# Sketch attention and causal experts on one core: TensorE's order written out, normalisation moved to the values, two sketch matmuls made one

## The chip, the cores and the metric

The kernel runs on one core of a Trainium2 chip. The metric is the device time of one execution in microseconds (us), the median of several runs. TensorE does matrix products and transposes, VectorE (DVE) and ScalarE (ACT) do reductions, exponentials and the copies out of PSUM, GpSimd (POOL) does small elementwise work in SBUF, and DMAs are issued by SyncE's queue and ScalarE's.

## The reference

There are four batches of 1088 tokens. A first part makes x from sketches of q and k, a second part runs four causal attention experts on x and mixes two of them for each token:

```python
phi(x) = outer(S1 x, S2 x)                 # 8 x 8 = 64 features, per head (4 heads of 32)
kv, z  = phi(k).T @ v, sum(phi(k))
x      = (phi(q) @ kv) / (phi(q) @ z + 1e-6)          # heads side by side: 128 wide
logits = x @ w_gate;  w = softmax over the two largest
for e in range(4):
    q, k, v = x @ wq[e], x @ wk[e], x @ wv[e]         # 64 wide
    a  = softmax(causal(q k.T / 8))                   # a / (a.sum() + 1e-9)
    out += gate weight of e * (a @ v @ wo[e])
```

S1 and S2 are float64 in the inputs. The kernel splits each into a nearest float32 (hi) and the rest (lo).

## The kernel before

All matrix products are float32. The program shows each such product as two MATMUL instructions, a transpose as one.

**First part of a batch** (`sketch_attention`, lines 216 to 268). k and q are brought to [128 = 4 heads x 32, tokens] by VectorE. `features` makes, for each of 9 chunks of 128 tokens, two accumulating products with the hi and the lo sketch (L200, 64 columns each), copies one half out of PSUM (L204) and lets VectorE multiply the halves (L209). `kv` is a sum over the chunks with two heads in one product (L236). Then follow, in three groups of three chunks, transposes of phi(q) (L246), their copy to SBUF, the numerators and denominators (L252), the division (L257 to L259) and transposes to xT (L264).

**Projections** (`project`, lines 271 to 315). Four products of 1088 columns for q and k of the experts (L277, L279), nine for v and the logits (L288), and the gate's weights on VectorE.

**Experts** (`experts`, lines 417 to 441). The 1088 queries are nine tiles: eight of 128 and a last one of 64. The steps run over groups of tiles (0 to 3, 4 to 7, 8), pairs of experts g and tiles i. `weights` (L321) makes the scores of two experts e (L336; each uses 64 of the array's rows), adds the causal mask by a product (L339), takes the row maximum (L345), scales it (L348), the exponential with its sum (L351), and multiplies the weights by gate over sum (L358 to L360). `turn_weights` (L372) transposes them in chunks of four, each chunk into one PSUM bank and out again by `evacuate` (lines L67 on VectorE, every third, and L69 on ScalarE). `values` (L385) multiplies them with v for up to 512 queries, the two experts at different columns of the array, and `output` (L396) applies wo.

**Order.** The loop at the end (lines 443 to 459) emits `weights` of a step, `turn_weights` of the step before, and one piece of the next batch's first part and projections. The framework's scheduler then orders each engine's instructions itself, TensorE's too. Of the eight PSUM banks, scores have two tiles of two banks, `tp` two banks and `o` two.

Of the kernel before, what the change touches and what calls it, by code (L numbers as in the profile page):

```python
# [9 lines left out]
F32 = mybir.dt.float32  # L10
# [8 lines left out]
def kernel(  # L19
# [37 lines left out]
    ps_o = ctx.enter_context(tc.tile_pool(name="ps_o", bufs=2, space=bass.MemoryType.PSUM))  # L57

    def const(name, shape, dt=F32):
        return cp.tile(shape, dt, name=name, tag=name)  # L60

# [9 lines left out]
    # ---- buffers of the first part: a batch's loads follow the reads of the one before it  # L71
# [8 lines left out]
    glog = const("glog", [128, NJ, E])  # L80
# [14 lines left out]
    # ---- the sketches: rows (S1, S2) at each head's partitions  # L95
# [8 lines left out]
    else:  # L104
# [9 lines left out]
        # The words of a float64, as a sum of two float32: the nearest one, and the rest. Both come  # L114
        # from its leading 24 bits, which are a float32, and its last 29.
# [38 lines left out]
    SK = []  # L154
    for n, s_sb in enumerate(sketches):
        ST = const(f"ST{n}", [128, 32])
        SK.append(const(f"SK{n}", [128, 2, H, R]))
        nc.vector.transpose(ST, s_sb)
        nc.vector.memset(SK[n], 0.0)
        for h in range(H):  # L160
            rows = slice(32 * h, 32 * h + 32)
            nc.vector.tensor_copy(SK[n][rows, :, h, :], ST[rows, 0 : 2 * R].rearrange("d (x r) -> d x r", x=2))  # L162
    NS = len(sketches)

# [5 lines left out]
    nc.gpsimd.memset(glog, 0.0)  # L170

    # ---- constants and weights of the second part
# [8 lines left out]
    for e in range(1, E):  # L181
        nc.gpsimd.memset(lower[:, e, 0:e], 1.0)

# [10 lines left out]
    # ---- first part of a batch, in pieces: x of its tokens, transposed  # L194
    def features(b, nm, xT_):
        """The products of two sketches, tokens on partitions; tokens that pad give zeros."""
        ab = ps_sc.tile([128, 1024], F32, tag="sc", name=f"{nm}ab{b}")
        for j in range(NJ):
            for s in range(NS):
                nc.tensor.matmul(ab[:, 64 * j : 64 * j + 64], xT_[:, 128 * j : 128 * j + 128],  # L200
                                 SK[s].rearrange("p x h r -> p (x h r)"), start=(s == 0), stop=(s == NS - 1))
        ab = ab[:, 0 : 64 * NJ].rearrange("p (j x m) -> p j x m", x=2, m=H * R)
        fa = p2.tile([128, NJ, H * R], F32, tag="fa", name=f"{nm}a{b}")
        nc.scalar.copy(fa, ab[:, :, 0])  # L204
        fp = p2.tile([128, NJ, H, R * R], F32, tag="fp", name=f"{nm}p{b}")
        fa4 = fa.rearrange("p j (h r) -> p j h r", r=R)
        fb4 = ab[:, :, 1].rearrange("p j (h r) -> p j h r", r=R)
        for h in range(H):
            nc.vector.tensor_tensor(  # L209
                out=fp[:, :, h].rearrange("p j (x y) -> p j x y", y=R),  # L210
                in0=fb4[:, :, h, None, :].to_broadcast([128, NJ, R, R]),
                in1=fa4[:, :, h, :, None].to_broadcast([128, NJ, R, R]),
                op=ALU.mult)
        return fp

    def sketch_attention(b, xT):
        n = NJ - 1
        nc.gpsimd.tensor_copy(vp[:, 0:n, :, 0:D].rearrange("p j h d -> p h j d"), vin)
        nc.gpsimd.tensor_copy(vp[0:64, n, :, 0:D], vtl)
        # Chunk j of k is the tokens that v has at vp[:, j]: c = j, n + j, 2 * n + j and 3 * n + j.  # L220
        nc.vector.transpose(kT[:, 0 : 128 * n].rearrange("p (j g t) -> p j g t", j=n, g=4),
                            kin[:, 0 : 128 * n].rearrange("p (g j d) -> p j g d", g=4, j=n))
        nc.vector.transpose(kT[:, 128 * n : S], kin[:, 128 * n : S])
        nc.vector.transpose(qT[:, 0:S], qin)
        if b + 1 < B:
            load(b + 1)
        kp = features(b, "k", kT)
        yield
        qp = features(b, "q", qT)
        yield  # L230

        kv = ps_o.tile([128, 512], F32, tag="o", name=f"kv{b}")
        kv = kv[:, 0 : 4 * (D + 1)].rearrange("p (m h d) -> p m h d", m=2, h=2)
        for m in range(2):
            for j in range(NJ):
                nc.tensor.matmul(kv[:, m], kp[:, j, 2 * m : 2 * m + 2, :].rearrange("p h f -> p (h f)"),  # L236
                                 vp[:, j, 2 * m : 2 * m + 2, :], start=(j == 0), stop=(j == NJ - 1))
        for h in range(2):
            nc.scalar.copy(kvz[64 * h : 64 * h + 64, :, h, :], kv[64 * h : 64 * h + 64, :, h, :])
        yield  # L240

        for g in range(NJ // 3):
            tq = ps_sc.tile([128, 1024], F32, tag="sc", name=f"tq{b}_{g}")
            for y in range(6):
                x, m = divmod(y, 2)
                nc.tensor.transpose(tq[:, 128 * y : 128 * y + 128],  # L246
                                    qp[:, 3 * g + x, 2 * m : 2 * m + 2, :].rearrange("p h f -> p (h f)"), ident)
            qpT = p2.tile([128, 6, 128], F32, tag="qpT", name=f"qpT{b}_{g}")
            evacuate(qpT.rearrange("p y s -> p (y s)"), tq[:, 0:768])
            num = ps_o.tile([128, 512], F32, tag="o", name=f"num{b}_{g}")  # L250
            for y in range(6):
                nc.tensor.matmul(num[:, 66 * y : 66 * y + 66], qpT[:, y], kvz[:, y % 2].rearrange("p h d -> p (h d)"),  # L252
                                 start=True, stop=True)
            nu = num[:, 0 : 12 * (D + 1)].rearrange("p (m d) -> p m d", d=D + 1)
            den = p2.tile([128, 12], F32, tag="den", name=f"den{b}_{g}")
            xs = p2.tile([128, 3, 128], F32, tag="xs", name=f"xs{b}_{g}")
# [5 lines left out]
            tx = ps_tp.tile([128, 512], F32, tag="tp", name=f"tx{b}_{g}")  # L262
            for x in range(3):
                nc.tensor.transpose(tx[:, 128 * x : 128 * x + 128], xs[:, x], ident)  # L264
# [3 lines left out]
            yield  # L268

    # ---- projections and gate of a batch, in pieces  # L270
    def project(b, xT, qk, vt, gw):
        tail = ps_o.tile([128, 512], F32, tag="o", name=f"qkt{b}")
        for a in range(2 * NG):
            w = wqk[:, a // NG, 2 * (a % NG) : 2 * (a % NG) + 2, :].rearrange("p e d -> p (e d)")
            t = ps_sc.tile([128, 1024], F32, tag="sc", name=f"qk{b}_{a}")
            for c in range(2):
                nc.tensor.matmul(t[:, 512 * c : 512 * c + 512], w, xT[:, 512 * c : 512 * c + 512],  # L277
                                 start=True, stop=True)
# [211 lines left out]
```

## Time and profile before

| | |
|---|---|
| median of three runs | 732.28 us (727.87 to 733.38) |
| span of the profiled execution | 731.8 us |
| TensorE busy | 632.2 us, 3012 matmul instructions |
| TensorE weight loads busy | 396.9 us |
| VectorE busy | 373.3 us |
| ScalarE busy | 231.1 us |
| GpSimd busy | 7.2 us |
| mean granted TensorE clock | 0.80 |

The span is from the first to the last instruction of one execution. The page gives no other time for that execution, and the span is within 0.1% of the median of the runs, so a sum made against the span can be read as one against the median. Busy times are unions over an engine; matmuls overlap one another in the array, so a busy TensorE isn't one at its peak. The granted clock is a share of 2.4 GHz and takes two levels, 0.5 (1.2 GHz) and 1.0.

### The profile page before, as it was taken

Reading aid. Unit: us, or ns where it says so; the run is one execution under the profiler, and the core shown is the slowest. Engines: PE = TensorE matmul, PEld = TensorE weight load, DVE = VectorE, ACT = ScalarE, POOL = GpSimd, SP = SyncE. Lnnn points to the kernel's source line nnn. Section 1 sums busy time; section 2 is a strip of 40 time slices with the busy share of each in tenths; the row PEclk is TensorE's granted clock in tenths of the full one; section 3 lists DMA queues with packets and bytes.
Section 4 is the critical chain, followed back from the end, with each engine's and each line's share of the span. In section 5 each row is a group of like instructions: output and inputs, shape, how many; then the busy total and the mean of one; then the engine's idle time right before and its main releaser. Section 6 shows DMA issues by size and latency. Waiting matters only on the chain.

```text
span 731.8 us, 8068 instructions
## 1 busy us (share of the span) xinstructions
PE 632.2 (86%) x3012; PEld 396.9 (54%) x3012; DVE 373.3 (51%) x1107; ACT 231.1 (32%) x555; POOL 7.2 (1%) x26
## 2 busy tenths in 40 slices
PE   3988999999878999898879899999888887888696
PEld 2965866554435885554434687554443553544345
DVE  4425454566563235658672334546755345574622
ACT  0022123343342113434341412344433333343413
POOL 1000000000000000000000000000000000000000
PEclk9989557999688555999987655999967867898885
DMA  7110110000000000000000000000000000000000
GB/s 211 57 36 1 46 47 1 0 15 0 1 0 15 3 1 0 1 14 1 1 0 1 16 1 1 1 3 12 1 1 0 15 3 0 16 0 1 0 11 6
DMA packets 11318, 9.97 MB, mean 14 GB/s; under 512 B 3600, under 2 KB 10256, under 8 KB 11280
## 3 DMA queue, kind: packets, MB, share of 16 engines
q1 hardware_dynamic: 9152, 8.92, 4.1%
q10 hardware_dynamic: 2128, 0.54, 0.4%
q8 instruction: 24, 0.39, 0.2%
q14 instruction: 14, 0.11, 0.1%
HBM read 7.23 MB, written 2.23 MB: 13 GB/s over the span
## 4 chain that ended last, share of the span: by engine, by line
PE 77%; DVE 11%; ACT 8%; issue 2%; DMA 1%; SPq 0%; ACTq 0%; DVEq 0%
PE sc L336 22%; PE av L385 14%; PE tp L372 12%; DVE mx L345 5%; ACT a L351 4%; PE qk L277 4%; PE qab L200 4%; PE kv L236 4%; PE kab L200 4%; ACT aT L69 3%; PE po L396 3%; PE num L252 3%; PE sc L339 2%; PE vg L288 2%; PE tq L246 2%
## 5 line engine op out<-in xcount | busy, mean ns | idle before, releaser
L336 PE MATMUL sc<-qkT 64*128 64x512 f32 (+3 forms) x448 | 195.1, 643 | 44.5 <-ACT a L351 44.2
L345 DVE TENSOR_REDUCE mx<-sc 128x1 f32<-128x128 f32 (+8 forms) x144 | 112.4, 804 | 141.8 <-PE sc L339 104.8
L372 PE MATMUL tp<-ident,a 128*128 128x128 f32 (+1 forms) x720 | 134.1, 326 | 25.9 <-ACT aT L69 17.0
L69 ACT COPY aT<-tp 128x256 f32<-128x256 f32 (+4 forms) x159 | 70.1, 449 | 205.9 <-PE tp L372 204.0
L351 ACT ACTIVATE a<-sc,mx 128x128 f32<-128x128 f32 (+8 forms) x144 | 112.0, 782 | 73.0 <-DVE mx L348 52.6
L372 PEld LDWEIGHTS tp<-ident,a 128*128 128x128 f32 (+1 forms) x720 | 95.7, 175 | 66.9 <-ACT aT L69 30.6
L336 PEld LDWEIGHTS sc<-qkT 64*128 64x128 f32 (+1 forms) x448 | 71.5, 212 | 101.8 <-ACT a L351 61.1
L385 PE MATMUL av<-aT,vt 128*64 128x64 f32 (+5 forms) x672 | 108.3, 443 | 1.5 <-DVE mx L348 1.5
L360 DVE TENSOR_SCALAR a<-a,z,gw 128x128 f32<-128x128 f32 (+8 forms) x144 | 86.8, 604 | 3.6
L385 PEld LDWEIGHTS av<-aT,vt 128*64 128x64 f32 (+1 forms) x672 | 54.1, 179 | 50.3 <-issue 37.3
L67 DVE COPY aT<-tp 128x512 f32<-128x512 f32 (+4 forms) x81 | 41.4, 511 | 38.1 <-PE tp L372 36.5
L200 PE MATMUL kab<-SK,kT 128*128 128x64 f32 x144 | 28.9, 389 | 16.6 <-DVE SK L162 12.6
L339 PEld LDWEIGHTS <-identb 128*128 128x128 bf16 (+1 forms) x144 | 11.0, 101 | 50.4 <-issue 47.9
L200 PEld LDWEIGHTS kab<-SK,kT 128*128 128x128 f32 x144 | 28.0, 300 | 17.5 <-DVE SK L162 12.8
L277 PE MATMUL qk<-xT,wqk 128*128 128x512 f32 x64 | 33.0, 638 | 0.9 <-issue 0.9
L236 PE MATMUL kv<-vp,kp 128*128 128x66 f32 x144 | 32.2, 417 | 0.0
L236 PEld LDWEIGHTS kv<-vp,kp 128*128 128x128 f32 x144 | 31.9, 333 | 0.0
L358 DVE TENSOR_SCALAR z<-z 128x1 f32<-128x1 f32 (+1 forms) x144 | 21.1, 147 | 21.0 <-ACT a L351 20.3
L200 PE MATMUL qab<-SK,qT 128*128 128x64 f32 x144 | 31.7, 421 | 0.0
L200 PEld LDWEIGHTS qab<-SK,qT 128*128 128x128 f32 x144 | 31.3, 333 | 0.0
L69 ACT COPY yT<-av 128x512 f32<-128x512 f32 (+1 forms) x17 | 8.1, 476 | 66.1 <-PE av L385 66.1
L351 ACT ACTIVATION_READ_ACCUMULATOR a<-sc,mx 128x1 f32 (+1 forms) x144 | 28.7, 200 | 0.0
(103 smaller groups left out, 413.3 us busy)
## 6 DMA issues: line engine op xcount, KB each, us to landing
kin<-in_k_dram SPq DMA_DIRECT2D x4, 544.0 KB, 4.7
qin<-in_q_dram SPq DMA_DIRECT2D x4, 544.0 KB, 6.1
vin<-in_v_dram SPq DMA_DIRECT2D x16, 128.0 KB, 3.6
out_dram<-ob SPq DMA_DIRECT2D x8, 256.0 KB, 2.3
wqk<-in_moe_wq_dram ACTq DMA_DIRECT2D x1, 128.0 KB
S_raw<-in_S_dram ACTq DMA_DIRECT2D x8, 2.0 KB
wqk<-in_moe_wk_dram ACTq DMA_DIRECT2D x1, 128.0 KB, 3.2
wvg<-in_moe_wv_dram ACTq DMA_DIRECT2D x1, 128.0 KB
```

The source lines that it names most:

```text
L67: nc.vector.tensor_copy(out_, in_)
L69: nc.scalar.copy(out_, in_)
L200: nc.tensor.matmul(ab[:, 64 * j : 64 * j + 64], xT_[:, 128 * j : 128 * j + 128], SK[s].rearrange("p x h r -> p (x h r)"), start=(s == 0), ...
L236: nc.tensor.matmul(kv[:, m], kp[:, j, 2 * m : 2 * m + 2, :].rearrange("p h f -> p (h f)"), vp[:, j, 2 * m : 2 * m + 2, :], start=(j == 0), ...
L277: nc.tensor.matmul(t[:, 512 * c : 512 * c + 512], w, xT[:, 512 * c : 512 * c + 512], start=True, stop=True)
L336: nc.tensor.matmul(dest(e, c0, c1), qk[rows, g, 128 * i : 128 * i + nq], qk[rows, NG + g, c0:c1], start=True, stop=(c1 < n))
L339: nc.tensor.matmul(dest(e, 128 * i, n), identb[:, 0:nq], cmask[:, 0:nq], start=False, stop=True)
L345: nc.vector.reduce_max(mx[0:nq, x : x + 1], dest(e, c0, c1), axis=AX.X)
L351: nc.scalar.activation(out=a[0:nq, c0:c1], in_=dest(e, c0, c1), func=ACTF.Exp, bias=mx[0:nq, 0:1], scale=scale, accum_out=z[0:nq, x : x + 1])
L360: nc.vector.tensor_scalar(out=a[0:nq, 0:n], in0=a[0:nq, 0:n], scalar1=z[0:nq, 0:1], scalar2=gw[0:nq, i, c : c + 1], op0=ALU.mult, op1=ALU. ...
L372: nc.tensor.transpose(tp[0 : size(j), j - j0, 0:nq], ats[e][0:nq, 128 * j : 128 * j + size(j)], ident[0:nq, 0:nq])
L385: nc.tensor.matmul(av[HD * e : HD * e + HD, lo:w], vt[0 : size(j), j, c : c + HD], aTs[e][0 : size(j), j, lo:w], start=(j == 0), stop=(j = ...
```

## The change

TensorE's instructions now run in the order in which the program emits them (`manual_schedule` for that engine alone; the other engines are still ordered by the scheduler). A batch is 17 units: tiles 0 to 7 by pairs p of tiles and pairs g of experts, then one last unit with tile 8 of all four experts, two of them at output partitions 0 to 63 and two at 64 to 127. In each round of the loop TensorE gets the scores of a unit, then the transposes of the unit before in chunks of four, with pieces of the next batch's first part between them (by given costs), second halves of values and outputs, and at the end the first half of the values of a pair that is complete.

The weights stay unnormalised. Gate over sum is computed per pair, widened on GpSimd, transposed on TensorE (`gates`), and multiplied on the values as they leave PSUM. The score's scale goes into wq once. Hi and lo sketches are one product of 128 columns, copied to SBUF and added there; the feature products are GpSimd's, but for k of the first batch. `kv` is made a head at a time. PSUM: scores as before, `tp` two banks, `o` one, and one bank `f` for the pieces, the gates and the outputs (the first batch's pieces go round `o`, `tp` and `f`).

```diff
-    ps_o = ctx.enter_context(tc.tile_pool(name="ps_o", bufs=2, space=bass.MemoryType.PSUM))
+    ps_o = ctx.enter_context(tc.tile_pool(name="ps_o", bufs=1, space=bass.MemoryType.PSUM))
+    ps_f = ctx.enter_context(tc.tile_pool(name="ps_f", bufs=1, space=bass.MemoryType.PSUM))
...
+        def sketch(nm, xT_, j0):
...
+            t = bank(f"{nm}ps{b}_{j0}")
+            for j in range(j0, j1):
+                nc.tensor.matmul(t[:, w * (j - j0) : w * (j - j0) + w], xT_[:, 128 * j : 128 * j + 128],
+                                 SKW.rearrange("p s x h r -> p (s x h r)"), start=True, stop=True)
+            evacuate(abS[nm][:, j0:j1].rearrange("p j s m -> p (j s m)"), t[:, 0 : w * (j1 - j0)])
+        def products(nm, eng):
...
+                nc.gpsimd.tensor_tensor(out=t[:, :, 0], in0=t[:, :, 0], in1=t[:, :, 1], op=ALU.add)
...
+            for h in range(H):
+                eng.tensor_tensor(
+                    out=fp[:, :, h].rearrange("p j (x y) -> p j x y", y=R),
...
+                for x in range(2):
+                    h = 2 * m + x
+                    nc.tensor.matmul(kv[64 * x : 64 * x + 64, m], kp[:, j, h], vp[:, j, h, :],
+                                     start=(j == 0), stop=(j == NJ - 1))
...
+        pieces = [(0.0, begin)]
+        pieces += [(0.9, lambda j=j: sketch("k", kT, j)) for j in range(0, NJ, NB)]
+        pieces += [(0.0, lambda: products("k", kq))]
+        pieces += [(0.9, lambda j=j: sketch("q", qT, j)) for j in range(0, NJ, NB)]
+        pieces += [(0.0, lambda: products("q", nc.gpsimd))]
+        pieces += [(2.0, lambda: (kvs(0), kvs(1)))]
+        pieces += [(0.5, lambda y=y: turn_features(y)) for y in range(0, 2 * NJ, 4)]
+        pieces += [(1.3, lambda g=g: numer(g)) for g in range(NJ // 3)]
+        pieces += [(0.4, lambda g=g: turn_x(g)) for g in range(NJ // 3)]
+        pieces += [(0.5, lambda j=j: project_v(j)) for j in range(NJ)]
+        pieces += [(0.0, gate)]
+        pieces += [(0.9, lambda a=a, c=c: project(a, c)) for c in range(2) for a in (0, 2, 1, 3)]
+        pieces += [(0.5, project_tails)]
...
+        if n <= 512:
+            t = ps_sc.tile([128, 2, 512], F32, tag="sc", name=f"sc{b}_{i}_{g}")
...
+        for e in range(2):
+            if n > 512:
+                nc.vector.tensor_reduce(mx[:, e : e + 1], sc[e][:, 0:n], axis=AX.X, op=ALU.max, negate=True)
+            soften(ats[e][:, 0:n], sc[e][:, 0:n], mx[:, e : e + 1], z[:, e : e + 1])
...
-            nc.vector.tensor_scalar_add(z[0:nq, 0:1], z[0:nq, 0:1], 1e-9)
-            nc.vector.reciprocal(z[0:nq, 0:1], z[0:nq, 0:1])
-            nc.vector.tensor_scalar(out=a[0:nq, 0:n], in0=a[0:nq, 0:n], scalar1=z[0:nq, 0:1],
-                                    scalar2=gw[0:nq, i, c : c + 1], op0=ALU.mult, op1=ALU.mult)
...
+    def gates(name, z, gws, w):
...
+        nc.vector.tensor_scalar_add(r, z, 1e-9)
+        nc.vector.reciprocal(r, r)
...
+        nc.gpsimd.tensor_tensor(out=rb[:, 0 : w // 128].rearrange("p x (e d) -> p x e d", d=HD),
+                                in0=gws[:, :, :, None].to_broadcast(wide), in1=r[:, :, :, None].to_broadcast(wide),
+                                op=ALU.mult)
+        t = ps_f.tile([128, 512], F32, tag="f", name=f"rt{name}")
+        for x in range(w // 128):
+            nc.tensor.transpose(t[:, 128 * x : 128 * x + 128], rb[:, x], ident)
+        rs = p4.tile([128, 256], F32, tag="rs", name=f"rs{name}", bufs=2)
+        nc.scalar.copy(rs[:, 0:w], t[:, 0:w])
...
+                def close(p=p, g=g, yT=yT, z=z, name=name, values=values):
+                    rs = gates(name, z, gw[:, 2 * p : 2 * p + 2, 2 * g : 2 * g + 2], 256)
+                    values(0, p + 1)
+                    def rest():
+                        values(p + 1, 2 * p + 2)
+                        av = values.__defaults__[-1][0]
+                        nc.vector.tensor_tensor(out=yT[:, g], in0=av[:, 0:256], in1=rs, op=ALU.mult)
+                        if g == NG - 1:
+                            later.append(lambda: output(b, p, yT))
+                    later.append(rest)
...
+    with tc.manual_schedule(engines={mybir.EngineType.PE}):
...
+            share = sum(c for c, _ in pieces) / (2 * NJ - 1)
+            for n, (make, turned, close) in enumerate(units(b, *now)):
+                ats = make()
+                jobs = turns or []
+                ready = list(later)
+                later.clear()
+                gaps = max(len(jobs), 2)
+                for s in range(gaps):
+                    if s < len(jobs):
+                        jobs[s]()
+                    if ready and s:
+                        ready.pop(0)()
+                    spend(share / gaps)
+                for f in ready:
+                    f()
+                if after:
+                    after()
+                turns, after = turned(ats), close
```

## Rows read from the trace of the kernel before

**Rows 1.** The page: span, granted clock in 40 slices, chain by line.

```profile
span 731.8 us, 8068 instructions
...
PEclk9989557999688555999987655999967867898885
...
PE sc L336 22%; PE av L385 14%; PE tp L372 12%; DVE mx L345 5%; ACT a L351 4%; PE qk L277 4%; PE qab L200 4%; PE kv L236 4%; PE kab L200 4%; ACT aT L69 3%; PE po L396 3%; PE num L252 3%; PE sc L339 2%; PE vg L288 2%; PE tq L246 2%
```

**Rows 2.** Busy time of each engine by stretch: one first part, two batches, all stretches summed.

```profile
15.00:69.00 54.00, 48.68 (x218) 39.18 (x217) 21.13 (x60) 9.24 (x19) 1.29 (x2) 0.94 0.16 44
...
244.00:416.00 172.00, 154.10 (x758) 97.18 (x760) 93.13 (x269) 56.59 (x139) 1.29 (x2) 0.80 0.01 4
...
590.00:732.00 142.00, 113.61 (x568) 64.17 (x566) 71.66 (x206) 49.85 (x125) 0.00 (x0) 0.79 0.02 5
sum 732.00, PE 632.19 PEld 396.90 DVE 373.33 ACT 231.15 POOL 7.25; mean PE 105.37 PEld 66.15 DVE 62.22 ACT 38.52 POOL 1.21
```

**Rows 3.** The page's groups of instructions by line (busy us, mean ns, idle before).

```profile
L336 PE MATMUL sc<-qkT 64*128 64x512 f32 (+3 forms) x448 | 195.1, 643 | 44.5 <-ACT a L351 44.2
...
L372 PE MATMUL tp<-ident,a 128*128 128x128 f32 (+1 forms) x720 | 134.1, 326 | 25.9 <-ACT aT L69 17.0
...
L385 PE MATMUL av<-aT,vt 128*64 128x64 f32 (+5 forms) x672 | 108.3, 443 | 1.5 <-DVE mx L348 1.5
L360 DVE TENSOR_SCALAR a<-a,z,gw 128x128 f32<-128x128 f32 (+8 forms) x144 | 86.8, 604 | 3.6
...
L200 PE MATMUL kab<-SK,kT 128*128 128x64 f32 x144 | 28.9, 389 | 16.6 <-DVE SK L162 12.6
...
L236 PE MATMUL kv<-vp,kp 128*128 128x66 f32 x144 | 32.2, 417 | 0.0
...
L200 PE MATMUL qab<-SK,qT 128*128 128x64 f32 x144 | 31.7, 421 | 0.0
```

**Rows 4.** Timeline: scores of one expert, of both together, and the maxima after these.

```profile
125.41 1.12 PE L336 MATMUL sc<-qkT 64*128 64x512 f32 x2
...
665.53 1.56 PE L336 MATMUL sc<-qkT 64*128 64x512 f32 x8
...
667.29 1.82 DVE L345 TENSOR_REDUCE mx<-sc 128x1 f32<-128x768 f32 x2 [6.65 <-PE sc L339]
```

**Rows 5.** The chain in order of time: start, us, what.

```profile
117.80 2.57 PE num L252 x12
...
248.74 7.94 PE kab L200 x36
...
303.65 1.34 PE num L252 x12
...
409.57 2.31 PE av L385 x34
```

**Rows 6.** Busy time by stretch (PE, PEld, DVE, ACT, POOL, granted clock), two stretches.

```profile
250.00:285.00 35.00, 34.10 (x134) 27.71 (x134) 14.20 (x35) 5.80 (x17) 1.29 (x2) 0.50 0.00 0
300.00:360.00 60.00, 54.34 (x271) 30.34 (x271) 40.23 (x118) 24.64 (x54) 0.00 (x0) 1.00 0.02 5
```

**Rows 7.** The transposes of L372 alone, same view.

```profile
300.00:360.00 60.00, 11.73 (x78) 8.50 (x78) 1.00 0.02 5
```

**Rows 8.** Groups by line and shape, of ScalarE, VectorE and GpSimd.

```profile
L69 ACT COPY aT<-tp 128x512 f32<-128x512 f32 x63 | 36.7, 586 | 115.7 <-PE tp L372 115.7
...
L345 DVE TENSOR_REDUCE mx<-sc 128x1 f32<-128x1024 f32 x16 | 18.8, 1219 | 12.0 <-PE sc L339 12.0
L351 ACT ACTIVATE a<-sc,mx 128x1024 f32<-128x1024 f32 x16 | 17.7, 1115 | 0.1
...
L209 DVE TENSOR_TENSOR kp<-kab,ka 128x576 f32<-128x576 f32 x16 | 11.0, 750 | 5.3 <-ACT ka L204 5.1
...
L218 POOL COPY vp<-vin 128x1024 f32<-128x1024 f32 x4 | 4.2, 1056 | 262.3 <-PE kv L236 252.9 <-DMA wo<-in_moe_wo_dram 9.4
```

**Rows 9.** Waits by line, longest first: engine, line, waited for, us, times, longest.

```profile
PE sc L336 <- ACT a L351: 44.2, 36, 3.1
```

More of the change, by code (lines that the diff above doesn't have):

```diff
@@ L1 @@
+import collections
 import math
@@ L182 @@
         nc.gpsimd.memset(lower[:, e, 0:e], 1.0)
+    vts = [const(f"vt{n}", [128, NJ, E * HD + E]) for n in range(2)]
+    for t in vts:
+        nc.gpsimd.memset(t[64:, NJ - 1, E * HD :], 0.0)
     wqk = const("wqk", [128, 2, E, HD])
@@ L332, in weights, with scores @@
+    def scores(b, i, g, qk, z):
+        n = 128 * i + 128
+        if n <= 512:
+            t = ps_sc.tile([128, 2, 512], F32, tag="sc", name=f"sc{b}_{i}_{g}")
+            sc = [t[:, e, :] for e in range(2)]
+        else:
+            sc = [ps_sc.tile([128, 1024], F32, tag="sc", name=f"sc{b}_{i}_{g}_{e}") for e in range(2)]
         for c0 in range(0, n, 512):
@@ new lines, in scores_last, with turns_of, some @@
+            a = p4.tile([128, S], F32, tag="a", name=f"a{b}_8_{e}")
+            soften(a[:, 0:1024], sc[e], mx[:, 0:1], zz[:, 0:1])
+            soften(a[:, 1024:], ext[e][:, 0:64], mx[:, 0:1], zz[:, 1:2])
+            nc.vector.tensor_tensor(out=z[:, e : e + 1], in0=zz[:, 0:1], in1=zz[:, 1:2], op=ALU.add)
+            ats.append(a)
+        return ats
+    def turns_of(name, i, ats, aT, q0):
+        def some(k0, k1):
+            tp = ps_tp.tile([128, 4, 128], F32, tag="tp", name=f"tp{name}_{k0}")
+            nk = size(k0 // 2)
+            for k in range(k0, k1):
+                j, e = divmod(k, 2)
+                nc.tensor.transpose(tp[0:nk, k - k0, :], ats[e][:, 128 * j : 128 * j + nk], ident)
+            evacuate(aT[0:nk, k0:k1, q0 : q0 + 128], tp[0:nk, 0 : k1 - k0, :])
+        full = 2 * min(i + 1, NJ - 1)
+        cuts = [(k, min(k + 4, full)) for k in range(0, full, 4)]
+        if i == NJ - 1:
+            cuts.append((full, full + 2))
+        return [lambda k0=k0, k1=k1: some(k0, k1) for k0, k1 in cuts]
@@ L394, in output @@
+    def output(b, p, yT):
+        nq, n = (128, 2) if p < NJ // 2 else (64, 1)
+        po = ps_f.tile([128, 512], F32, tag="f", name=f"po{b}_{p}")
         for x in range(n):
@@ L443 @@
-    now, pieces = prepare(0)
-    for _ in pieces:
-        pass
-    waiting = None
-    for b in range(B):
-        coming, pieces = prepare(b + 1) if b + 1 < B else (None, iter(()))
-        for n, (make, use) in enumerate(experts(b, *now)):
-            ats = make()
-            if waiting is not None:
-                waiting[0](waiting[1])
-            waiting = (use, ats)
-            if n:
-                next(pieces, None)
-        for _ in pieces:
-            pass
-        now = coming
@@ L459 @@
-    waiting[0](waiting[1])
+    with tc.manual_schedule(engines={mybir.EngineType.PE}):
+        now, pieces = prepare(0)
+        for _, f in pieces:
+            f()
+        turns = after = None
+        for b in range(B):
+            coming, pieces = prepare(b + 1) if b + 1 < B else (None, [])
+            fill.extend(pieces)
+            share = sum(c for c, _ in pieces) / (2 * NJ - 1)
[12 more added lines that the diff above has]
+                for f in ready:
+                    f()
+                if after:
+                    after()
+                turns, after = turned(ats), close
+            spend(1e9)
+            now = coming
+        for f in turns:
+            f()
+        while later:
+            later.popleft()()
+        after()
+        while later:
+            later.popleft()()
```

397 lines of the change are left out of this document (205 added, 192 removed).

## The prediction

> **What bounds the kernel now.** I read the chain that ended last first. It is TensorE's: of the lines in [rows 1] the scores hold 22%, values 14%, transposes 12%, the maxima on VectorE 5% and the exponentials 4%. The busy times by stretch [rows 2] agree. In a steady batch TensorE is busy 154 of 172 us, VectorE 93, ScalarE 57. So VectorE and ScalarE have room, and what counts is how long TensorE is busy and why it isn't.
>
> Two things make TensorE's time long, and neither is the arithmetic.
>
> The first is the clock. The slices of the granted clock [rows 1] go up and down, and its mean is 0.80. With levels of 0.5 and 1.0 that is 2 x 0.20 x 731.8 = 293 us at the lower level. [Rows 6] show where: 250 to 285 us is busy throughout (34.1 of 35 us) and yet at 0.50, and that is where sketches and kv are made; 300 to 360 us stands at 1.00. The numerators' twelve instructions take 2.57 us in one place and 1.34 in another [rows 5]; that is the price of the level.
>
> The second is how the scores run. The two experts use different halves of the array's rows. One expert's 512 columns alone take 1.12 us, so both one after the other take 2.24, or 4.4 ns a column. Elsewhere eight instructions for both, of a tile whose maxima are over 768 columns, take 1.56 us, or 2.03 ns a column [rows 4]. The same work costs half where the two stand beside each other in TensorE's order. The scheduler often puts them apart, since the first buffer comes free before the second.
>
> Of TensorE's idle 99.6 us (731.8 - 632.2), 44.2 stand before scores that wait for the exponentials of an earlier tile to release their buffers [rows 9].
>
> **Scores: -90.** With the order fixed, both experts follow each other in every chunk. Tiles 0 to 7 have 128 x (1 + ... + 8) = 4608 columns for each g, 9216 a batch. The last unit has 1088, if its four products at four quarters of the array run together. That makes 10,304 x 2.03 ns = 20.9 us, 83.7 for four batches at the full clock, and at 0.80 it is 105 against 195.1 [rows 3]. If the four run only by twos it is 11 more. If no pairs ran together the gain would be nothing; the paired row speaks against that.
>
> **Transposes: -13, and +13 for the gates.** Tile 8's weights of both g are now stacked, so 18 of 180 transposes a batch go: 72 x 0.186 us (134.1 / 720, [rows 3]) = 13.4. The gates add 17 a batch, 68 x 0.186 = 12.7. The two cancel.
>
> **Sketches: -30.** 288 instructions [rows 3] become 144 with 128 columns instead of 64. 36 of the old ones take 7.94 us, 221 ns each [rows 5]. In that stretch weight loads are busy 27.7 of 35 us [rows 6], and the numerators, with a 128 x 128 weight and 66 columns, have the same spacing at this clock (214 ns): I take the load as what spaces them, so that the wider product costs nothing more. Half of 60.6 us goes. If columns set the spacing it would be nothing; I keep 0 to 30 for the range.
>
> **kv: -13.** 144 instructions become 288 with 64 x 33 work, two heads at different columns of the array. The nearest row is the values of the last tile, 64 columns and two at a time: 34 in 2.31 us, 68 ns each [rows 5]. 288 x 68 ns = 19.6 against 32.2. The far ends are 68 x 33/64 = 35 ns (22 gained) and the numerators' 112 ns (no gain).
>
> **Values and output: 0.** Groups of 256 queries instead of 512 need the same number of columns. Twice the instructions of half the length stay above the 68 ns.
>
> **Waits: -44.** Tiles up to 512 wide now put both experts in one buffer, so the next unit has the second one free. For wide tiles the next scores do wait for both exponentials: two maxima of 1.22 us and an exponential of 1.12 [rows 8], some 3.9 us with the small gaps. Ahead of that wait in TensorE's order stand up to 16 transposes (16 x 0.186 = 3.0 us), values and pieces, so it is covered in the first three batches. In the last batch no pieces are left; up to 1 us shows in each of its 8 wide units, which the next part takes in. The transposes no longer wait for the normalisation, 86.8 us of VectorE [rows 3], of which nothing was on the path but its latency.
>
> **New waits: +12.** TensorE can't pass over a blocked instruction any more; everything behind it waits. Three places are new. First, the pieces of a batch (36), the gates and the outputs share one PSUM bank, and each use ends with a copy of 0.59 us on ScalarE or one like it on VectorE [rows 8]; a batch has some 50 uses in about 120 us, so the bank is free most of the time, but the copy can stand behind an exponential. Second, the feature products on GpSimd. No row shows GpSimd with two inputs. Its copy of 1024 columns takes 1.056 us [rows 8], 0.59 us for 576, and twice that if inputs are read one after the other: 0.6 to 1.2 us for each of five instructions, 3 to 6 us from the last sketch of q to the first transpose of phi(q). kv stands between and covers about 5. Third, the gates' product queues behind these on GpSimd, and its two transposes block TensorE: up to 4.8 us, twice a batch. From nothing to 45 us in all; I take 12, nearer to the lower end, since GpSimd is idle for most of a batch. On VectorE the product of values and gate waits for the gates' copy, and behind it queue the maxima; its time replaces a copy.
>
> What the Trainium skill adds: "GPSIMD Engine Reference", section "Engine selection", puts two-input elementwise work on GpSimd at about half VectorE's speed. By that and VectorE's 0.75 us for the product [rows 8] it is 1.5 us and the sum would be some 10 us higher. No run here shows it yet.
>
> **Clock: -25.** Of 293 us at the lower level, some 43 go with sketches and kv, 36 with the scores (0.4 of 90) and 18 with the waits; 196 stay. Each 10 us of these that move to the upper level give back 5. The sketch stretch is broken up among products of more columns, and the gaps before scores go; I let 50 us move. The bounds are 0 and all of it, 98.
>
> **Sum.** 732 - 90 - 13 + 13 - 30 - 13 - 44 + 12 - 25 = 542 us. VectorE and ScalarE stay far below: VectorE loses the 86.8 us from its 373.3, ScalarE's 231.1 gains copies. A change of 1% is about what this kernel's runs can tell from none, as they spread over 0.8%.
>
> **Rivals.** *The clock falls* (chance 0.10). Pieces of 33 to 128 columns are now spread through the whole batch, between transposes, so the long stretches at 1.00 could break. If 100 us of the work at the upper level falls to the lower, it costs 100 and the 25 aren't gained: 667 us. For: 250 to 285 us is busy and slow. Against: 300 to 360 us holds pieces of that kind, and 11.7 us of transposes [rows 7], at 1.00. The Trainium skill, "TensorE: Matmul & The Clock Gate", section "PE-mode transpose", says that transposes don't engage the full clock as matmuls do. These 60 us don't contradict it, as other products stand between.
>
> *TensorE waits for copies* (0.05; slower). If each of the some 170 uses of bank `f` (36 pieces in three batches, 9 in the first, 36 gates, 20 outputs) stalls the ordered TensorE for an exponential ahead of the copy and the copy itself, 1.1 + 0.6 = 1.7 us, that is 290 us instead of 12: 820 us. It makes the kernel slower from a mean stall of 1.2 us a use: (732 - 530) / 170. For: two engines serve both exponentials and copies in order. Against: ScalarE is busy a third of a batch [rows 2].
>
> *The pairs don't run together* (0.07), so that the order does nothing for the scores: 542 + 90 = 632.
>
> *The clock stays up* (0.12). If all 196 us move and the new waits are nothing: 542 - 73 - 12 = 457.
>
> **How the numbers follow.** My forecast, 500 to 585 us, has 0.62: 542 with the sketches' 30, kv's ends, the waits' 0 to 45 and half of the clock's bounds. 0.04 stays for what I don't see. The range that holds 8 in 10 reaches into the rivals on both sides, 475 to 630. Faster by over 1%: 0.94; the waits for copies and part of the unseen make 0.04 for slower, and 0.02 is left for no change.
>
> **What would show it.** After the change the scores' group should be near 100 us with the same number of instructions, sketches near 30, kv near 20, the wait of scores for exponentials under 15, TensorE's busy time near 475, the mean clock near 0.84. Wrong would be: a clock under 0.75, TensorE waiting for copies or GpSimd for more than 50 us, or scores that stay above 150.

## The result and the profile after

The changed kernel takes 554.5 us in the median (550.8 to 559.7); against 732.35 us of before the ratio is 0.7563 (0.7523 to 0.7603). The profiled execution took 555.5 us, its span is 553.8. Now and then a run of a kernel stands a per cent or more above its fastest; all ratios here leave such runs out, but the profile of the run with two sketch products is of one.

The page: span, busy time of each engine, granted clock in 40 slices, chain by line.

```profile
span 553.8 us, 8147 instructions
...
PE 445.4 (80%) x3264; PEld 287.5 (52%) x3264; DVE 228.8 (41%) x486; ACT 230.3 (42%) x556; POOL 71.3 (13%) x99
...
PEclk9978979999997998799999898889799899999979
...
PE sc L392 14%; PE av L501 12%; PE tp L441 9%; ACT a L378 5%; PE qk L320 5%; PE vg L332 4%; DVE mx L402 3%; PE num L295 3%; PE rt L462 3%; POOL qp L256 3%; PE po L551 2%; PE sc L395 2%; PE av L533 2%; PE kps L244 2%; ACT aT L74 2%
```

TensorE's groups by line (busy us, mean ns, idle before and what ended it), where [rows 3] answer to the first ones.

```profile
L441 PE MATMUL tp<-ident,a 128*128 128x128 f32 (+1 forms) x648 | 106.8, 294 | 21.3 <-ACT a L378 17.0
L392 PE MATMUL sc<-qkT 64*128 64x512 f32 (+3 forms) x384 | 89.9, 553 | 0.8 <-ACT a L378 0.8
L501 PE MATMUL av<-aT,vt 128*64 128x256 f32 (+1 forms) x640 | 82.0, 388 | 0.0
...
L462 PE MATMUL rt<-ident,rb 128*128 128x128 f32 x68 | 15.6, 309 | 27.4 <-POOL rb L457 7.3 <-DVE xs L302 3.6 <-ACT qkT L74 2.2
L286 PE MATMUL tq<-ident,qp 128*128 128x128 f32 x72 | 13.9, 322 | 13.6 <-POOL qp L256 8.5 <-ACT qpT L74 2.2 <-ACT kvz L277 1.7
L244 PE MATMUL kps<-SKW,kT 128*128 128x128 f32 x72 | 12.1, 319 | 14.4 <-DVE SKW L165 13.6 <-DVE kab L72 0.8
L533 PE MATMUL av<-aT,vt 128*64 128x64 f32 (+1 forms) x288 | 11.2, 227 | 0.0
L244 PE MATMUL qps<-SKW,qT 128*128 128x128 f32 x72 | 11.1, 299 | 2.9 <-DVE ob L72 1.0 <-ACT ob L74 1.0 <-DVE kab L72 0.8
L273 PE MATMUL kv<-vp,kp 128*64 128x33 f32 x288 | 9.7, 224 | 0.6 <-DVE kp L256 0.4
L415 PE MATMUL sc<-qkT 64*64 64x512 f32 x64 | 8.1, 602 | 0.0
```

TensorE's busy time fell by 187 us, from 632.2 to 445.4. Scores went from 195 (198 with the last 64 columns, a group of their own) to 99 (89.9 + 8.1 and 1.4), transposes from 134 to 107, sketches from 61 to 23, kv from 32 to 10, values from 108 to 93 although they are the same columns. The clock has a part in all of them: its mean is 0.929 now, from 0.80. Time at the lower level was 2 x 0.20 x 731.8 = 293 us and is 2 x 0.071 x 553.8 = 79.

Idle time did not fall. It was 99.6 us and is 108.4. The 44 us before scores [rows 9] are gone (0.8 left), and in their place stand the gates' transposes (27.4), those of phi(q) (13.6) and small waits before almost every piece. The transposes of the weights wait about as long as before (21.3 against 25.9), but for exponentials instead of copies.

The longest of these waits, in the timeline of the last unit of batch 0:

```profile
162.94 1.95 PE L415 MATMUL sc<-qkT 64*64 64x512 f32 x16
...
164.93 2.36 DVE L424 TENSOR_REDUCE mx<-sc 128x1 f32<-128x1024 f32 x2 [2.31 <-PE sc L415]
...
167.73 1.11 ACT L378 ACTIVATE a<-sc,mx 128x1024 f32<-128x1024 f32 x1 [4.09 <-DVE mx L426]
...
168.83 0.31 ACT L378 ACTIVATE a<-ext,mx 128x64 f32<-128x64 f32 x1
...
169.28 1.11 PE L441 MATMUL tp<-ident,a 128*128 128x128 f32 x4 [4.09 <-ACT a L378]
```

The last unit's scores put their final 64 columns into both `tp` banks. The transposes of the unit before it are ready, but have no bank until an exponential has read these columns: 4.1 us in which TensorE does nothing, once a batch. Behind it the granted clock is 0.50 and four transposes take 1.11 us; elsewhere, at the upper level, four take 0.60.

The trace holds the clock's level from step to step, so TensorE's busy time can be split by it: 275 us of it stood at the lower level before, 67 do now. Counting these as half gives an estimate of the work as it would be at the upper level; it takes the two levels' times as 2 to 1, where the four transposes above have 1.11 to 0.60. By this the work fell from 495 to 412 us, by 83, and what the lower level costs on top fell from 137 to 34, by 104. More than half of what TensorE's busy time gained is the clock. Four of the runs below only move instructions, banks or elementwise work, and their work comes out at 412 to 415 us, which speaks for the estimate.

### The profile page after: what moved, and what is told of

It reads as the page before. It is cut to its first block, busy times and chain, and to the rows that moved or that the text cites. A ratio compares the mean times of both kernels' runs of the same rounds, so it can differ in the third digit from the quotient of the medians.

```text
span 553.8 us, 8147 instructions
## 1 busy us (share of the span) xinstructions
PE 445.4 (80%) x3264; PEld 287.5 (52%) x3264; DVE 228.8 (41%) x486; ACT 230.3 (42%) x556; POOL 71.3 (13%) x99
## 4 chain that ended last, share of the span: by engine, by line
PE 63%; DVE 14%; ACT 10%; issue 5%; POOL 5%; DMA 1%; ACTq 0%; POOLq 0%; DVEq 0%
PE sc L392 14%; PE av L501 12%; PE tp L441 9%; ACT a L378 5%; PE qk L320 5%; PE vg L332 4%; DVE mx L402 3%; PE num L295 3%; PE rt L462 3%; POOL qp L256 3%; PE po L551 2%; PE sc L395 2%; PE av L533 2%; PE kps L244 2%; ACT aT L74 2%
## 5 line engine op out<-in xcount | busy, mean ns | idle before, releaser
L441 PE MATMUL tp<-ident,a 128*128 128x128 f32 (+1 forms) x648 | 106.8, 294 | 21.3 <-ACT a L378 17.0
L378 ACT ACTIVATE a<-sc,mx 128x1024 f32<-128x1024 f32 (+7 forms) x136 | 103.0, 763 | 48.6 <-DVE mx L399 18.0
L74 ACT COPY aT<-tp 128x512 f32<-128x512 f32 (+2 forms) x121 | 64.2, 541 | 131.5 <-PE tp L441 131.0
L402 DVE TENSOR_REDUCE mx<-sc 128x1 f32<-128x640 f32 (+3 forms) x64 | 62.6, 1020 | 87.4 <-PE sc L395 87.4
L392 PE MATMUL sc<-qkT 64*128 64x512 f32 (+3 forms) x384 | 89.9, 553 | 0.8 <-ACT a L378 0.8
L501 PE MATMUL av<-aT,vt 128*64 128x256 f32 (+1 forms) x640 | 82.0, 388 | 0.0
L392 PEld LDWEIGHTS sc<-qkT 64*128 64x128 f32 x384 | 36.8, 198 | 38.0 <-issue 32.9
L501 PEld LDWEIGHTS av<-aT,vt 128*64 128x64 f32 x640 | 41.9, 142 | 26.9 <-issue 13.1
L72 DVE COPY aT<-tp 128x512 f32<-128x512 f32 (+2 forms) x59 | 37.6, 639 | 28.7 <-PE tp L441 28.4
L462 PE MATMUL rt<-ident,rb 128*128 128x128 f32 x68 | 15.6, 309 | 27.4 <-POOL rb L457 7.3
L378 ACT ACTIVATION_READ_ACCUMULATOR a<-sc,mx 128x1 f32 x136 | 27.3, 201 | 0.0
L286 PE MATMUL tq<-ident,qp 128*128 128x128 f32 x72 | 13.9, 322 | 13.6 <-POOL qp L256 8.5
L244 PE MATMUL kps<-SKW,kT 128*128 128x128 f32 x72 | 12.1, 319 | 14.4 <-DVE SKW L165 13.6
```

The source lines that it names most:

```text
L72: nc.vector.tensor_copy(out_, in_)
L74: nc.scalar.copy(out_, in_)
L378: nc.scalar.activation(out=dst, in_=src, func=ACTF.Exp, bias=mx, accum_out=z)
L392: nc.tensor.matmul(sc[e][:, c0:c1], qk[rows, g, 128 * i : 128 * i + 128], qk[rows, NG + g, c0:c1], start=True, stop=(c1 < n))
L402: nc.vector.tensor_reduce(mx[:, e : e + 1], sc[e][:, 0:n], axis=AX.X, op=ALU.max, negate=True)
L441: nc.tensor.transpose(tp[0:nk, k - k0, :], ats[e][:, 128 * j : 128 * j + nk], ident)
```

## The experiments

Theories: A, the order carries the gain, since it puts the two experts' scores side by side; B, the order is worth nothing without the rest. Times are ratios to the kernel before on the same chip; with 732 us the changed kernel's 0.756 is 554.

**The order alone**, in the kernel before:

```diff
-    now, pieces = prepare(0)
-    for _ in pieces:
-        pass
+    with tc.manual_schedule(engines={mybir.EngineType.PE}):
+        now, pieces = prepare(0)
+        for _ in pieces:
+            pass
...
```

> The kernel before, with nothing changed but that TensorE runs in the order in which the program emits its instructions. Theory A (the order carries most of the gain, since it puts the two experts' scores side by side): the scores' group falls from 195 us busy to about 105, and the time falls to some 640 to 700 us, less than the full 90 us, since TensorE now also waits at blocked instructions that the scheduler passed over. Theory B (the order is worth nothing without the shorter work and the new places of the pieces): the scores' group still falls, but TensorE's idle time grows from 100 us by as much or more, and the time is 730 us or above.

Measured: 1.064 (1.060 to 1.067), slower. TensorE's groups:

```profile
L336 PE MATMUL sc<-qkT 64*128 64x512 f32 (+3 forms) x448 | 159.9, 660 | 32.7 <-ACT a L351 21.5 <-DVE qp L209 5.6 <-DVE kT L223 3.6
L372 PE MATMUL tp<-ident,a 128*128 128x128 f32 (+1 forms) x720 | 131.9, 329 | 61.0 <-ACT a L351 32.1 <-ACT aT L69 25.1 <-DVE aT L67 1.3
```

And two tiles with 1024 columns in its timeline, both at the upper level:

```profile
571.36 1.99 PE L336 MATMUL sc<-qkT 64*128 64x512 f32 x8
...
600.10 2.97 PE L336 MATMUL sc<-qkT 64*128 64x512 f32 x8 [1.46 <-ACT a L351]
```

B holds. Scores did become shorter, but by 35 us and not by 90. They keep 21.5 us of waits for exponentials, and the tile behind such a wait takes 2.97 us instead of 1.99: in it the second expert's first product starts 0.99 us after the first's, so these two don't run together. By the program the reason is the second expert's buffer, which comes free later than the first's. TensorE's idle time rose from 100 to 163 us (779.0 - 616.2); 35 of these 63 us came before transposes (61 against 25.9 in [rows 3]).

**The order free again**, in the changed kernel:

```diff
-    with tc.manual_schedule(engines={mybir.EngineType.PE}):
+    if True:
```

> The changed kernel, with TensorE's order left to the scheduler again; all else as changed. Theory A: the scheduler pulls the experts' scores of wide tiles apart, their group rises from 99 us to 140 or more, waits before scores come back, and the time is 600 to 640 us. Theory B (the shorter work alone makes the gain): the time stays within 2% of 554 us.

Measured: 0.741 (0.737 to 0.745), so 543 us and 2% faster than with the order fixed. That is the lower edge of B's range; neither theory said that the free order would be faster. The page:

```profile
span 540.3 us, 8155 instructions
...
PE 497.9 (92%) x3264; PEld 300.4 (56%) x3264; DVE 228.3 (42%) x486; ACT 230.8 (43%) x556; POOL 71.4 (13%) x99
```

And TensorE's groups:

```profile
L392 PE MATMUL sc<-qkT 64*128 64x512 f32 (+3 forms) x384 | 135.3, 545 | 3.2 <-ACT a L378 3.2
L441 PE MATMUL tp<-ident,a 128*128 128x128 f32 (+1 forms) x648 | 103.6, 287 | 3.8 <-ACT a L378 2.7 <-DVE aT L72 0.8
```

The scheduler does pull some pairs apart (scores 135 against 90, A's part of it), and it fills most waits: TensorE idles 42 us instead of 108. The fixed order buys some 50 us of busy time and pays some 66 of idle. Counted at the upper level, the scores are 140 us here against 92 as changed and 154 in the kernel before: most of their work was saved by the order. The mean clock is 0.95 here, so the clock rose without the order too.

**The experts' scores one after the other**, order fixed:

```diff
-        for c0 in range(0, n, 512):
-            for e in range(2):
+        for e in range(2):
+            for c0 in range(0, n, 512):
...
-        for e in range(2):
             nc.tensor.matmul(sc[e][:, 128 * i : n], identb, cmask, start=False, stop=True)
...
```

(The last unit's scores also run one expert after the other.)

> The changed kernel, order fixed, but each expert's scores in all chunks and its mask before the other expert's. Theory A (two experts side by side cost half): the scores' group rises from 99 us to 170 to 185, and the time by 60 to 80 us, to 615 to 635. Rival: the time is hidden behind waits that TensorE has anyway, and the kernel stays under 580.

Measured: 0.912 (0.906 to 0.918), 114 us more than as changed. The clock on the page, the groups of scores and masks, and one expert's 1024 columns in the timeline:

```profile
PEclk9799579999979956558998897655999989699999
```

```profile
L392 PE MATMUL sc<-qkT 64*128 64x512 f32 (+3 forms) x384 | 187.7, 601 | 0.0
...
L394 PE MATMUL sc<-cmask,identb 128*128 128x128 bf16 x128 | 31.3, 244 | 0.0
```

```profile
151.86 1.98 PE L392 MATMUL sc<-qkT 64*128 64x512 f32 x4
```

One expert's 1024 columns take as long as both experts' do together (1.99 us in the timeline of the order alone). The masks are bf16 products of one instruction each, the one exception to float32 in both kernels. The price of a broken pair is larger than I said: this group rises by 98 us and all scores from 99 to 211 (18.7 and 4.4 for the last unit), where 170 to 185 was expected, and the mean clock falls from 0.93 to 0.86. By the same estimate as above, the work rises by 79 us, the cost of the lower level by 53, and idle time falls by 21. So side-by-side scores are worth more than 100 us here. Whether a fixed order is needed for them is another question, to which the runs in the scheduler's order come back.

**Two sketch products again**:

```diff
-                nc.tensor.matmul(t[:, w * (j - j0) : w * (j - j0) + w], xT_[...], SKW..., start=True, stop=True)
+                for s in range(NS):
+                    o = w * (j - j0) + 64 * s
+                    nc.tensor.matmul(t[:, o : o + 64], xT_[...], SKW[:, s]..., start=True, stop=True)
```

> The changed kernel with hi and lo sketches as two products of 64 columns again, each to its own columns, all else as changed. Theory A (the weight load spaces these products, so the wider one costs nothing more): the sketches' group rises from 23 us to about 42 and the time by 12 to 20 us, to 567 to 575. Rival (columns space them): the group and the time stay, 555.

Measured: 0.790 (0.786 to 0.794), 24 us more. The group:

```profile
L246 PE MATMUL qps<-SKW,qT 128*128 128x64 f32 x144 | 28.9, 384 | 2.3 <-ACT ob L74 1.0 <-DVE ob L72 0.9 <-DVE kab L72 0.4
...
L246 PE MATMUL kps<-SKW,kT 128*128 128x64 f32 x144 | 23.9, 334 | 13.4 <-DVE SKW L165 12.6 <-DVE kab L72 0.8
```

It is 53 us instead of 23, in a profiled execution of 591.8 us with a mean clock of 0.90. Four chunks of k, at the upper level in both runs, here and as changed:

```profile
352.37 1.90 PE L246 MATMUL kps<-SKW,kT 128*128 128x64 f32 x16
```

```profile
185.35 1.06 PE L244 MATMUL kps<-SKW,kT 128*128 128x128 f32 x8
```

The product of 128 columns costs no more than that of 64, as predicted. That the columns don't space these products is shown; that the weight load does is still an argument.

**Normalisation on the weights again**, order fixed; `gates` is gone:

```diff
+        for e in range(2):
+            normalise(ats[e][:, 0:n], z[:, e : e + 1], gw[:, i, 2 * g + e : 2 * g + e + 1])
...
-                    rs = gates(name, z, gw[:, 2 * p : 2 * p + 2, 2 * g : 2 * g + 2], 256)
...
-                        nc.vector.tensor_tensor(out=yT[:, g], in0=av[:, 0:256], in1=rs, op=ALU.mult)
+                        evacuate(yT[:, g], av[:, 0:256])
```

> The changed kernel with gate over sum multiplied on the weights again by VectorE, before the transposes, and without the gates' product on GpSimd, their transposes and their copy. Theory A (the normalisation was never on the path, as predicted; the gates cost TensorE 16 us busy and 27 us of waits): the time falls by 10 to 30 us, to 525 to 545. Rival (VectorE's 90 us of normalisation delay the maxima behind them, and with these the exponentials and the transposes that now must come in order): the time rises to 575 or more, and TensorE's idle time with it.

Measured: 0.725 (0.720 to 0.730), 23 us faster than as changed, though VectorE is busy 320 us instead of 229. The transposes of the weights:

```profile
L451 PE MATMUL tp<-ident,a 128*128 128x128 f32 (+1 forms) x648 | 107.3, 293 | 33.8 <-ACT a L378 17.6 <-DVE a L384 7.1 <-DVE z L382 6.7
```

They now wait some 14 us for the normalisation (L382 and L384), so in this order it is on the path. The gates' transposes cost more: 15.6 us busy and 27.4 of waits. Moving the normalisation to the values, with the gates at this place in the order, cost time.

**Feature products on VectorE**, with the sketches' sum:

```diff
-                nc.gpsimd.tensor_tensor(out=t[:, :, 0], in0=t[:, :, 0], in1=t[:, :, 1], op=ALU.add)
+                nc.vector.tensor_tensor(out=t[:, :, 0], in0=t[:, :, 0], in1=t[:, :, 1], op=ALU.add)
...
-        kq = nc.vector if first else nc.gpsimd
+        kq = nc.vector
...
-        pieces += [(0.0, lambda: products("q", nc.gpsimd))]
+        pieces += [(0.0, lambda: products("q", kq))]
```

> The changed kernel with the sum of the sketches and all feature products on VectorE instead of GpSimd. Theory A (the queue on GpSimd is a new wait: 8.5 us before the transposes of phi(q), 7.3 before the gates' transposes, and lower clock after them): the time falls by 12 to 20 us, to 535 to 543. Rival (the 30 us of products on VectorE delay maxima by as much): the time stays within 1% of 554.

Measured: 0.756 (0.753 to 0.759), no difference. The waits stay and change their names: the gates' transposes wait 9.2 us for GpSimd, those of phi(q) 5.7 for VectorE. In all the gates' transposes wait 29.0 us (27.4 as changed) and those of phi(q) 9.8 (13.6). So the queue of feature products on GpSimd was not what the gates waited for, and phi(q) waits for its products on either engine.

**Gates' transposes later**, behind the second half of the values:

```diff
                     def rest():
                         values(p + 1, 2 * p + 2)
+                        rt = rs()
...
-                        nc.vector.tensor_tensor(out=yT[:, g], in0=av[:, 0:256], in1=rs, op=ALU.mult)
+                        nc.vector.tensor_tensor(out=yT[:, g], in0=av[:, 0:256], in1=rt, op=ALU.mult)
```

> The changed kernel with the gates' two transposes and their copy moved behind the second half of the pair's values, some 5 us later in TensorE's order; the sums and the product on GpSimd stay where they were. Theory A (these transposes wait 27 us in all because they come right after the copy of a piece and, at the start of a batch, behind the feature products): most of that goes, and the time falls by 12 to 25 us, to 530 to 543. Rival (the waits are for bank f and only move with the transposes): within 1% of 554.

Measured: 0.722 (0.717 to 0.727), 25 us faster than as changed, with the sums and the product where they were. The gates' transposes:

```profile
L463 PE MATMUL rt<-ident,rb 128*128 128x128 f32 x68 | 15.0, 297 | 4.6 <-POOL rb L457 1.4 <-ACT qpT L74 0.8 <-ACT xT L74 0.6
```

So the loss lay in the place of two transposes in the order. Of their 27.4 us of waits 4.6 are left, but pieces now wait 11.6 for the gates' copy out of bank `f`: idle time fell by 13 us (108.4 to 95.5). The other 10 are busy time, at a mean clock of 0.95 instead of 0.93.

**The last unit's columns in `o` and `f`**:

```diff
-        ext = [ps_tp.tile([128, 512], F32, tag="tp", name=f"ext{b}_{e}") for e in range(2)]
+        ext = [ps_o.tile(...), ps_f.tile(...)]
...
-            share = sum(c for c, _ in pieces) / (2 * NJ - 1)
+            share = sum(c for c, _ in pieces) / (2 * NJ - 2) + 0.01
```

> The changed kernel with the last 64 score columns of the last unit in banks o and f instead of the two tp banks, and the pieces spread over 16 units instead of 17, so that none needs bank f meanwhile. Theory A (the longest waits of TensorE, 4.1 us in each batch, are the transposes of the unit before waiting for the tp banks that these columns hold until their exponential): 2 to 4 us and the drop of the clock behind it go in each batch, the time falls by 8 to 20 us, to 534 to 546. Rival (something else is late right there, as bank f): within 1% of 554.

Measured: 0.753 (0.749 to 0.757), no clear difference. The transposes' group, and the longest new wait:

```profile
L441 PE MATMUL tp<-ident,a 128*128 128x128 f32 (+1 forms) x648 | 98.2, 281 | 7.6 <-DVE aT L72 3.9 <-ACT aT L74 3.0 <-DVE mx L426 0.4
```

```profile
PE rt L462 <- ACT a L378: 9.4, 4, 3.1
```

The transposes' wait fell from 21 to 8 us, so the banks were its cause. But the gates' transposes, next in order, now wait for bank `f` until the same exponential.

**Both of these together**:

```diff
-        ext = [ps_tp.tile([128, 512], F32, tag="tp", name=f"ext{b}_{e}") for e in range(2)]
+        ext = [ps_o.tile(...), ps_f.tile(...)]
...
+                        rt = rs()
```

> The changed kernel, order fixed, with the gates' transposes behind the second half of the values (529.5 us alone) and the last unit's last 64 columns in banks o and f (552 alone). Theory (the second gave little because the gates' transposes then waited for bank f, 9.4 us; with these moved its 8 to 12 us come): 515 to 523. Rival (the wait for the last unit's exponentials just moves to the next thing in order): 527 to 532.

Measured: 0.721 (0.713 to 0.728), as the gates' place alone. The rival's time holds, but not its reason. TensorE's waits for exponentials are 4 us in all here (3.4 before values) against 17 with the gates' place alone, so they did go. Idle time fell by only 4 us (95.5 to 91.7), as waits for the gates' copy (16.4 us against 11.6) and for other copies of pieces came in their place. The pieces also stand in other places of the order here; which of the two moved these waits isn't shown.

**Pieces in lumps**, order free: 11 lumps, one behind each unit from the second on, instead of pieces spread by cost:

```diff
-                    spend(share / gaps)
...
+                if n and fill:
+                    fill.popleft()[1]()
```

> The changed kernel with TensorE's order left to the scheduler (544 us so far), and the pieces of the next batch emitted in 11 lumps, one behind each unit from the second on, as the kernel before did, instead of spread over the chunks by their costs. Theory C (with the order free, spreading the pieces is what keeps TensorE busy and its clock up; lumps of narrow products bring back the stretch at the lower level at the start of a batch): the mean clock falls from 0.95 to 0.85 or less and the time rises by 25 to 50 us, to 570 to 595. Rival D (the scheduler mixes the pieces anyway, and the gain lies in the shorter work and the banks): within 2% of 544.

Measured: 0.749 (0.740 to 0.757) against 0.741: not clearly slower, and the clock is 0.95. Spreading the pieces explains little of the gain.

**Pieces in the scores' tiles**, order free:

```diff
-            if not first or turns[0] % 4 == 0:
+            if not first:
+                return ps_sc.tile([128, 1024], F32, tag="sc", name=name)[:, 0:512]
+            if turns[0] % 4 == 0:
```

> The changed kernel with TensorE's order left to the scheduler (544 us so far), and the pieces of the next batch in the scores' tiles, as before, instead of their own bank f; they stay spread. Theory E (the pieces' own bank is what took the waits of scores for exponentials away, 44 us before, 3 us with the order free): waits of scores and of pieces come back, and the time rises by 20 to 60 us, to 565 to 605. Rival (two-bank tiles give the pieces two places instead of one, and the scores' wait stays hidden): within 2% of 544, or less.

Measured: 0.706 (0.699 to 0.713), 26 us faster than with bank `f`. Theory E has the wrong sign for the time. Some of its waits do come back: TensorE idles 58 us (512.8 - 454.9) against 42, 8.3 of it before projections that wait for exponentials.

```profile
L394 PE MATMUL sc<-qkT 64*128 64x512 f32 (+3 forms) x384 | 99.7, 526 | 0.9 <-ACT xT L74 0.4 <-ACT a L380 0.3 <-DVE qab L72 0.2
```

The scores are 100 us here and 135 with bank `f`, both in the scheduler's order: the pairs stay mostly together. TensorE's order in the traces shows it. Of 192 score products of tiles 0 to 7, 9 stand alone between other work here, 74 with bank `f`, 52 in the kernel before and none as changed. So a fixed order isn't needed for the pairs. Why the scheduler keeps them together here isn't shown.

**Order free, normalisation on the weights**:

```diff
-    with tc.manual_schedule(engines={mybir.EngineType.PE}):
+    if True:
...
-                    rs = gates(name, z, gw[:, 2 * p : 2 * p + 2, 2 * g : 2 * g + 2], 256)
```

> The changed kernel with TensorE's order left to the scheduler and gate over sum on the weights again. With the order fixed, the latter took 25 us off. Theory A (that gain was the gates' 16 us of transposes and some of their waits): with the order free the waits are hidden anyway, so only the 16 us come, 525 to 532. Rival (the scheduler needs VectorE's room for its reordering, or the gain was all waits): 540 or more.

Measured: 0.692 (0.686 to 0.698), 507 us on the scale above (509 in its own runs): the fastest version of this study, 8.5% under the changed kernel.

```profile
span 507.6 us, 8113 instructions
...
PE 466.9 (92%) x3196; PEld 284.5 (56%) x3196; DVE 320.1 (63%) x798; ACT 225.1 (44%) x544; POOL 51.5 (10%) x63
...
PEclk9979999999998999999999899999999799999989
```

It is faster than either theory said, 36 us under the order free alone. TensorE is busy 31 us less (466.9 against 497.9), 15 of them the gates' transposes, and idle as little (41 us). Pieces in the scores' tiles were not tried on top of it.

## Why the prediction was right, point by point

The time was forecast at 542 us and is 554. That it came so close is luck in part: the clock and the new waits were each off by some 40 us, in opposite directions. The table splits TensorE's span as above, with the work counted at the upper level. The forecast's row follows from its terms: 133 us of work go, 79 of them at the lower level, and 146 stay there. The work fell by 83 us where 94 were forecast.

| us | work | cost of the lower level | idle |
|---|---|---|---|
| before | 495 | 137 | 100 |
| forecast | 401 | 73 | 68 |
| as changed | 412 | 34 | 108 |
| as changed, order free | 472 | 26 | 42 |

- **Scores, -90.** Measured -99, of which 63 is work (154 to 92, counted at the upper level) and the rest clock. The reason given, "with the order fixed", holds for the work: with the order free it falls by 14, with the order alone by 33. But the pieces in the scores' tiles bring 44 in the scheduler's order, so a fixed order is one way to it and not the only one. The last unit's four products do run together: 1024 columns in 1.95 us, 1.9 ns a column.
- **Sketches -30, kv -13, transposes -13 and +13.** Measured -37, -22, -27 and +16. The sketches' step was tested by itself, 24 us. kv's 68 ns came from a row at the lower level, though the forecast didn't say so; as changed kv runs at the upper level, at 34 ns (9.7 us for 288). The transposes' term was wrong: counted at the upper level they are 98 us before and 97 now, so taking away 72 of 720 saved about 1 us, and the rest of the 27 is the clock. The values, with the same columns, are 87 us in both.
- **Clock, -25.** This was mis-sized. I let 50 of 196 us at the lower level move up; by the same split 117 did (196 - 79). What moved them is open: breaking the pairs of scores brings half of the lower level's cost back (34 to 87 us), the gates' place a tenth of it (34 against 22), and the clock is up with the order free as well.
- **Waits, -44 and +12.** The 44 went as described. The new ones were mis-sized: idle time ended at 108 us where 68 was forecast, so they are some 53, past the 45 that I gave as their upper end. The places named were right (bank `f`, GpSimd before phi(q)'s transposes, the gates), but I priced them as if the copy were mostly done in time. What I missed are the two `tp` banks held by the last unit, 17 us, and what the place of the gates' transposes costs, 25 us.
- **The signs of being wrong.** One of them came: counted by what ended them, TensorE's waits for copies are 47 us and for GpSimd 16, together more than 50. The time is within the range because the clock paid for it.
- **GpSimd.** The product of 576 columns takes 1.18 us (1.41 for the sum), at the upper end of 0.6 to 1.2. It didn't matter: the products on VectorE give the same time. By the Trainium skill, "GPSIMD Engine Reference", section "Engine selection", 1.5 us was the estimate. On VectorE the same product takes 0.75 to 0.86 us and the sum 0.75, so the measured ratios are 1.4 to 1.6 and 1.9: the Trainium skill's factor of about two fits the sum better than the product.
- **Rivals.** The clock rose instead of falling. Waiting for copies happened, at a small part of its price (47 us, not 290). The Trainium skill's sentence on transposes and the clock ("TensorE: Matmul & The Clock Gate", section "PE-mode transpose") stays untested: no run here has a stretch of transposes alone. That nothing of the normalisation was on the path but its latency holds in the scheduler's order, where TensorE's transposes wait about 1 us for it (before, and with it on the weights and the order free). In the changed kernel's fixed order it is 14 us, and the gates that replaced it cost 23 us more than that saved.

What stays open: of the some 190 us between the kernel before and the changed one with its order free, 23 are work, 111 the lower level's cost and 57 idle time, by the table. The sketches explain 24 of the gain (with the order fixed), and pieces in lumps or in the scores' tiles don't take it away. Undone one at a time were neither the last unit for four experts, nor kv by heads, nor the fused tiles of narrow scores, nor values by 256 queries. I can't divide the rest among them, nor say which of them moved the clock.

## What to carry to other kernels

Where two products can run side by side, make sure that they follow each other in TensorE's order and that the second one's buffer is free by then, and look at the group's busy time to see whether they do. Fixing an engine's whole order for that also gives up the filling of waits, so run the same kernel with the order free before keeping it. When a wait in a fixed order is removed, look at once at the next instruction in the order; twice here the gain was gone there. And split busy time by the clock's level before crediting a change with it: the transposes' 27 us were almost all clock.

## What the runs showed that I had not expected

With scores one expert at a time the mean clock is 0.86 instead of 0.93, although TensorE is busier (87% of the span against 80%); why isn't shown. And giving VectorE 91 us more work made the kernel faster in both orders. VectorE, busy 61 to 63% of the span with it, had the room, and TensorE lost the gates' transposes and, in the fixed order, their waits.
